# One activation instruction for a feed-forward's gate in 109 of its 256 units, tanh and a product in the other 147

## The chip, the cores and the metric

The kernel runs on one core of a Trainium2 chip. The metric is the device time of one execution in microseconds; the time before is the median of three runs. Five engines work side by side, each with its own queue of instructions and each waiting on the others through semaphores: PE (TensorE, the matmuls; PEld is its weight load), DVE (VectorE), ACT (ScalarE), POOL (GpSimd) and SP (SyncE, which here only issues DMAs).

## The reference

Three stages follow each other, all in float32:

```python
def _attn_ref(q, k, v, p):            # 8 batches, 8 heads, 576 tokens, head size 64
    p_packed = sm_attn(p, k, v)       # 32 packed queries
    return sm_attn(q, p_packed, p_packed)

def _moe_ref(x, w_in, w_out):         # 4608 tokens, 512 -> 2048 -> 512
    h = x @ w_in
    g = h * (1.0 / (1.0 + np.exp(-1.702 * h)))
    return (g @ w_out).astype(np.float32)

def _moe2_ref(x, w1, w2, w3, w_out):  # 512 -> 768 -> 512
    h = np.maximum(np.maximum(x @ w1, x @ w2), x @ w3)
    return (h @ w_out).astype(np.float32)
```

The change is in the gate of `_moe_ref`, the line `g = h * sigmoid(1.702 h)`.

## The kernel before

Every float32 product is made of three matmuls on a high and a low part of each operand (`mm3`, lines 100 to 102, the line numbers that most matmuls carry in the profile). So each left or right side has to be split: a copy into a rounded high part on ACT, then a subtraction for the low part, mostly on DVE.

The first feed-forward is cut into 256 **units**. A unit `n` is one batch, one half of its 576 tokens (288 columns) and one of 16 chunks of 128 of the 2048 hidden values. Three functions work on it:

- `h_unit(n)`: six matmuls of 288 columns into a PSUM tile `h` (two buffers, tag `ph`), then tanh(0.851 h) on ACT into `t` (line 460), then `t = (t + 1) * h` on DVE (line 461). This is twice the gated value, since sigmoid(1.702 h) is half of one plus that tanh. The product is the last reader of `h`.
- `g_unit(n)`: `t` is copied into the high part of `g` on ACT (line 466), and the low part is the difference (line 468), on DVE, for units 0 and 1 on POOL.
- `out_unit(n)`: twelve matmuls of 288 columns, which add `g` times a piece of `w_out` to four PSUM banks `acc`. After the last unit of a run of chunks the banks go to `x2` with a factor of one half (lines 488, 492 and 494), and a finished `x2` is written to DRAM.

In the plan, `out_unit(n - 2)` follows `h_unit(n)`, so a `g` has about two units' time to get ready. The attention of later batches and the conversion of weights run in between: softmax takes exponentials on ACT (lines 259 and 340), and `convert_low` and `conv_late` take the bit patterns of the weights apart with several DVE operations and a Relu with a bias on ACT (lines 154 and 520).

`main` lists all steps with due times and runs them in that order; each engine's queue is then put in order when the kernel is built, so a queue is not simply the program's text. Some instructions are tied behind the latest one of a kind: `sums` and `split_lo` behind `latest["dve"]`, `split_hi` behind `latest["act"]`.

From about 800 us on the second feed-forward runs, which the change does not touch.

Of the kernel before, what the change touches and what calls it, by code (L numbers as in the profile page):

```python
# [12 lines left out]
AF = mybir.ActivationFunctionType  # L13
ALU = mybir.AluOpType
# [29 lines left out]
def tile_packed_attention_moe(  # L44
# [13 lines left out]
    nc = tc.nc  # L58
# [19 lines left out]
    def f(t):  # L78
        return t.bitcast(F32)
# [11 lines left out]
    def x_tile(name, dt=F32):  # L91
        return up.tile([P, 4 * HALF], dt, tag="x", bufs=4, name=name)
# [5 lines left out]
    def mm3(o, a, b, start, stop, more=False):  # L98
        (ah, al), (bh, bl) = a, b
        nc.tensor.matmul(o, al, bh, start=start, stop=False, skip_group_check=more)  # L100
        nc.tensor.matmul(o, ah, bl, start=False, stop=False, skip_group_check=more)  # L101
        nc.tensor.matmul(o, ah, bh, start=False, stop=stop, skip_group_check=more)  # L102
# [313 lines left out]
    gt, acc = {}, {}  # L416
    latest = {}
# [30 lines left out]
        start.setdefault((b, fc // 4), n)  # L448
    part = {}

    def h_unit(n):
        b, hf, fc = units[n]
        o = ps_h.tile([P, TB], F32, tag="ph", name=f"h_{n}")[:, :HALF]
        hs = slice(hf * HALF, hf * HALF + HALF)
        fs = slice(fc % 4 * P, fc % 4 * P + P)
        for g in range(2):
            w = pw[b, fc // 4][:, g]
            mm3(o, (w[:, 0, fs], w[:, 1, fs]), [t[:, hs] for t in at[b, g]], g == 0, g == 1)
        t = gp.tile([P, HALF], F32, tag="t", name=f"t_{n}")
        nc.scalar.activation(t, o, AF.Tanh, scale=0.5 * 1.702)  # L460
        nc.vector.scalar_tensor_tensor(out=t, in0=t, scalar=1.0, in1=o, op0=ALU.add, op1=ALU.mult)  # L461
        gt[n] = t

    def g_unit(n):
        g = gp.tile([P, 2, HALF], F32R, tag="g", name=f"g_{n}")
        latest["act"] = nc.scalar.copy(g[:, 0], gt[n])  # L466
        eng = nc.gpsimd if n < 2 else nc.vector
        latest["dve"] = eng.tensor_tensor(out=g[:, 1], in0=gt[n], in1=f(g[:, 0]), op=ALU.subtract)  # L468
        gt[n] = g

    def out_unit(n):
        b, hf, fc = units[n]
        w = wo[fc]
        g = gt.pop(n)
        for dc in range(KD):
            if n in first:
                acc[dc] = ps_c.tile([P, TB], F32, tag=f"c{dc}", name=f"acc_{n}_{dc}")
            ds_ = slice(dc * P, dc * P + P)
            o = acc[dc][:, :HALF]
            mm3(o, (w[:, 0, ds_], w[:, 1, ds_]), (g[:, 0], g[:, 1]), n in first, n in last)  # L480
            if n not in last:
                continue
            if dc == 0:
                old = part.pop((b, hf), None)
                x2 = old or x_tile(f"x2_{n}")
                x2 = x2.rearrange("p (c t) -> p c t", c=KD)
            if old is not None:
                nc.vector.scalar_tensor_tensor(
                    out=x2[:, dc], in0=o, scalar=0.5, in1=x2[:, dc], op0=ALU.mult, op1=ALU.add
                )  # L490
            elif dc % 2 == 0:
                nc.scalar.mul(x2[:, dc], o, 0.5)
            else:
                nc.vector.tensor_scalar(out=x2[:, dc], in0=o, scalar1=0.5, scalar2=None, op0=ALU.mult)
        if n in last:
            if fc < NFC - 1:
                part[b, hf] = x2.rearrange("p c t -> p (c t)")
            else:
                c0 = b * S + hf * HALF
                nc.sync.dma_start(x2d[:, :, c0:c0 + HALF], x2)  # L500
# [303 lines left out]
    def main():  # L804
# [12 lines left out]
        for n in range(N1 + 2):  # L817
            tn[n] = t
            if n < N1:
                add(t, h_unit, n)  # L820
            if n >= 2:
                add(t + HU / 2, out_unit, n - 2)
            if n < N1:
                add(t + HU / 2 + .01, g_unit, n)
            t += (1.23 * HU) if n < 11 else HU * 1.16
# [181 lines left out]
```

## Time and profile before

| | us |
|---|---|
| median of three runs (1333.99 to 1334.6) | 1334.4 |
| the profiled execution's own time | 1333.64 |
| its span, first to last instruction | 1331.5 |
| PE busy in the span | 1308.8 |
| DVE busy in the span | 919.9 |
| ACT busy in the span | 533.3 |

The profile is one execution. Busy time is the union of an engine's instructions. A matmul of 288 columns is shown as some 0.3 us long, but they are pipelined, and one starts every 0.13 us; so PE can be shown busy while its queue loses a tenth of a microsecond, and losses are better read from the starts of its matmuls.

### The profile page before, as it was taken

The numbers are of one execution on the slowest core, as the hardware profiler recorded it, in microseconds if no ns is written. First come the engines' busy times: TensorE is split into PE (matmuls) and PEld (weight loads), VectorE is DVE, ScalarE is ACT, GpSimd is POOL, SyncE is SP. The second block draws the span as 40 slices with busy tenths as digits, with TensorE's granted clock in tenths as the row PEclk, the third lists the DMA queues.
The fourth block names the chain that finished last, engine by engine and source line by source line (L and its number), as shares of the span: only waits on it lengthen the run. The fifth ranks groups of instructions, "written<-read, shape, count | busy, mean of one in ns | idle before, by whom it ended". The sixth has DMA issues, their size and how long they took to land.

```text
span 1331.5 us, 22347 instructions
## 1 busy us (share of the span) xinstructions
PE 1308.8 (98%) x8614; PEld 1229.7 (92%) x8614; DVE 919.9 (69%) x1896; ACT 533.3 (40%) x1140; POOL 107.4 (8%) x218
## 2 busy tenths in 40 slices
PE   6899999999999999999999999999999999999998
PEld 5699898989999989999999999999899899999997
DVE  6899976874756565669999889736556467366461
ACT  3466544554445444446656442311311313123111
POOL 1200001100000000000000001001011011010000
PEclk9899999999999999999999999999999999999999
DMA  9697734643323331236655649847657476575451
GB/s 338 211 403 300 251 107 139 193 123 120 106 80 100 103 102 54 82 112 195 207 200 191 206 160 360 294 169 252 223 188 264 151 261 239 172 254 197 174 174 48
DMA packets 88875, 249.70 MB, mean 188 GB/s; under 512 B 10177, under 2 KB 39361, under 8 KB 81857
## 3 DMA queue, kind: packets, MB, share of 16 engines
q0 software_dynamic: 24640, 132.66, 29.2%
q1 hardware_dynamic: 64128, 115.62, 25.4%
q8 instruction: 68, 1.11, 0.3%
q14 instruction: 39, 0.31, 0.1%
HBM read 204.47 MB, written 43.78 MB: 186 GB/s over the span
## 4 chain that ended last, share of the span: by engine, by line
PE 92%; DVE 4%; DMA 2%; issue 1%; ACT 1%; SPq 0%; POOL 0%; ACTq 0%; DVEq 0%; POOLq 0%
PE acc L100 10%; PE p L101 10%; PE p L100 10%; PE p L102 10%; PE acc L102 10%; PE acc L101 9%; PE h L100 5%; PE h L102 5%; PE h L101 5%; PE accb L101 4%; PE accb L102 4%; PE accb L100 4%; PE pw L100 1%; PE pw L101 1%; PE pw L102 1%; PE pv L287 1%
## 5 line engine op out<-in xcount | busy, mean ns | idle before, releaser
L100 PE MATMUL acc<-g,wo 128*128 128x288 f32 x1024 | 303.6, 299 | 0.0
L102 PE MATMUL acc<-g,wo 128*128 128x288 f32 x1024 | 300.6, 294 | 0.0
L101 PE MATMUL acc<-g,wo 128*128 128x288 f32 x1024 | 299.6, 293 | 0.4 <-POOL g L468 0.3
L100 PEld LDWEIGHTS acc<-g,wo 128*128 128x128 f32 x1024 | 191.4, 188 | 10.5 <-issue 5.3
L101 PEld LDWEIGHTS acc<-g,wo 128*128 128x128 f32 x1024 | 192.2, 188 | 4.3 <-issue 1.0
L102 PEld LDWEIGHTS acc<-g,wo 128*128 128x128 f32 x1024 | 192.0, 188 | 1.6 <-issue 1.5
L460 ACT ACTIVATE t<-h 128x288 f32<-128x288 f32 x256 | 104.8, 410 | 181.7 <-PE h L102 179.8
L461 DVE SCALAR_TENSOR_TENSOR t<-t,h 128x288 f32<-128x288 f32 x256 | 114.7, 450 | 84.7 <-ACT t L460 83.3
L100 PE MATMUL h<-at,pw 128*128 128x288 f32 x512 | 155.2, 304 | 1.3 <-DVE t L461 1.1
L101 PE MATMUL h<-at,pw 128*128 128x288 f32 x512 | 151.7, 296 | 0.3 <-POOL at L125 0.3
L102 PE MATMUL h<-at,pw 128*128 128x288 f32 x512 | 151.3, 296 | 0.0
L466 ACT CAST g<-t 128x288 fp32r<-128x288 f32 x256 | 110.6, 433 | 93.6 <-DVE t L461 92.4
L468 DVE TENSOR_TENSOR g<-t,g 128x288 fp32r<-128x288 f32 x254 | 114.9, 453 | 34.7 <-ACT g L466 33.8
L681 DVE TENSOR_TENSOR u<-s,p 128x384 f32<-128x384 f32 x54 | 29.9, 553 | 119.1 <-PE p L102 119.1
L101 PE MATMUL p<-x_T,ws 128*128 128x384 f32 x324 | 108.2, 334 | 0.0
L100 PE MATMUL p<-x_T,ws 128*128 128x384 f32 x324 | 108.2, 334 | 0.0
L102 PE MATMUL p<-x_T,ws 128*128 128x384 f32 x324 | 108.1, 334 | 0.0
L100 PEld LDWEIGHTS h<-at,pw 128*128 128x128 f32 x512 | 96.3, 188 | 9.7 <-issue 5.6
L101 PEld LDWEIGHTS h<-at,pw 128*128 128x128 f32 x512 | 96.4, 188 | 1.7 <-POOL at L125 1.3
L102 PEld LDWEIGHTS h<-at,pw 128*128 128x128 f32 x512 | 96.4, 188 | 0.1
L711 ACT COPY s<-p 128x384 f32<-128x384 f32 x54 | 25.9, 479 | 161.8 <-PE p L102 161.7
L129 DVE TENSOR_TENSOR pw<-pw,pw 64x512 fp32r<-64x512 f32 (+1 forms) x110 | 74.9, 686 | 18.2 <-ACT pw L128 17.2
(175 smaller groups left out, 2637.1 us busy)
## 6 DMA issues: line engine op xcount, KB each, us to landing
ws<-wss POOLq DMA_DIRECT2D x54, 1024.0 KB, 7.6
wa<-wsa POOLq DMA_DIRECT2D x54, 768.0 KB, 4.6
wi<-wsc POOLq DMA_DIRECT2D x48, 512.0 KB, 3.9
k<-in_k SPq DMA_DIRECT2D x16, 576.0 KB, 4.2
q<-in_q SPq DMA_DIRECT2D x16, 576.0 KB, 3.9
x2d<-x SPq DMA_DIRECT2D x16, 576.0 KB, 4.0
wss<-ws SPq DMA_DIRECT2D x36, 256.0 KB, 4.0
xr<-x2d SPq DMA_DIRECT2D x24, 384.0 KB, 4.1
```

The costliest lines, as they stand in the source:

```text
L100: nc.tensor.matmul(o, al, bh, start=start, stop=False, skip_group_check=more)
L101: nc.tensor.matmul(o, ah, bl, start=False, stop=False, skip_group_check=more)
L102: nc.tensor.matmul(o, ah, bh, start=False, stop=stop, skip_group_check=more)
L129: nc.vector.tensor_tensor(out=lo, in0=o, in1=f(hi), op=ALU.subtract)
L287: self.mm = nc.tensor.matmul(o[x * D:x * D + D, :P], self.et[:, c * P + x * D:c * P + x * D + D], self.v[:, c, y * P:y * P + P], start=c = ...
L460: nc.scalar.activation(t, o, AF.Tanh, scale=0.5 * 1.702)
L461: nc.vector.scalar_tensor_tensor(out=t, in0=t, scalar=1.0, in1=o, op0=ALU.add, op1=ALU.mult)
L466: latest["act"] = nc.scalar.copy(g[:, 0], gt[n])
L468: latest["dve"] = eng.tensor_tensor(out=g[:, 1], in0=gt[n], in1=f(g[:, 0]), op=ALU.subtract)
L681: latest["dve"] = nc.vector.tensor_tensor(out=o, in0=a, in1=b, op=op)
L711: latest["act"] = nc.scalar.copy(self.s1, self.b1)
```

## The change

A unit is called direct when `10 <= n < 29`, `115 <= n < 129` or `n >= 180`: 19, 14 and 76 units, 109 of 256.

- In a direct unit, line 460 becomes one activation instruction whose function is h times sigmoid(1.702 h), and the DVE product of line 461 is not issued. `g_unit` copies and subtracts as before.
- In the other units `t` is still twice the gated value; the half is now applied in `g_unit`: the copy is a multiplication by 0.5 on ACT, and the subtraction a scalar-tensor-tensor operation on DVE.
- The factor of one half at `x2` goes: a scalar-tensor-tensor becomes a tensor-tensor addition, a multiplication by a constant becomes a copy.
- The low parts of units 0 and 1 move from POOL to DVE.
- `latest["act"]` is also set by the activation of a direct unit.

```diff
+    def direct(n):
+        return 10 <= n < 29 or 115 <= n < 129 or n >= 180
...
         t = gp.tile([P, HALF], F32, tag="t", name=f"t_{n}")
-        nc.scalar.activation(t, o, AF.Tanh, scale=0.5 * 1.702)
-        nc.vector.scalar_tensor_tensor(out=t, in0=t, scalar=1.0, in1=o, op0=ALU.add, op1=ALU.mult)
+        if direct(n):
+            latest["act"] = nc.scalar.activation(t, o, AF.Gelu_apprx_sigmoid)
+        else:
+            nc.scalar.activation(t, o, AF.Tanh, scale=0.5 * 1.702)
+            nc.vector.scalar_tensor_tensor(out=t, in0=t, scalar=1.0, in1=o, op0=ALU.add, op1=ALU.mult)
...
-        latest["act"] = nc.scalar.copy(g[:, 0], gt[n])
-        eng = nc.gpsimd if n < 2 else nc.vector
-        latest["dve"] = eng.tensor_tensor(out=g[:, 1], in0=gt[n], in1=f(g[:, 0]), op=ALU.subtract)
+        if direct(n):
+            latest["act"] = nc.scalar.copy(g[:, 0], gt[n])
+            latest["dve"] = nc.vector.tensor_tensor(out=g[:, 1], in0=gt[n], in1=f(g[:, 0]), op=ALU.subtract)
+        else:
+            latest["act"] = nc.scalar.mul(g[:, 0], gt[n], 0.5)
+            latest["dve"] = nc.vector.scalar_tensor_tensor(
+                out=g[:, 1], in0=gt[n], scalar=0.5, in1=f(g[:, 0]), op0=ALU.mult, op1=ALU.subtract
+            )
...
-                nc.vector.scalar_tensor_tensor(
-                    out=x2[:, dc], in0=o, scalar=0.5, in1=x2[:, dc], op0=ALU.mult, op1=ALU.add
-                )
+                nc.vector.tensor_tensor(out=x2[:, dc], in0=o, in1=x2[:, dc], op=ALU.add)
             elif dc % 2 == 0:
-                nc.scalar.mul(x2[:, dc], o, 0.5)
+                nc.scalar.copy(x2[:, dc], o)
             else:
-                nc.vector.tensor_scalar(out=x2[:, dc], in0=o, scalar1=0.5, scalar2=None, op0=ALU.mult)
+                nc.vector.tensor_copy(x2[:, dc], o)
```

## Rows read from the trace of the kernel before

**Rows 1.** The page's table of engines: busy us, share of the span, instructions.

```profile
PE 1308.8 (98%) x8614; PEld 1229.7 (92%) x8614; DVE 919.9 (69%) x1896; ACT 533.3 (40%) x1140; POOL 107.4 (8%) x218
...
PE 92%; DVE 4%; DMA 2%; issue 1%; ACT 1%; SPq 0%; POOL 0%; ACTq 0%; DVEq 0%; POOLq 0%
```

**Rows 2.** Busy time of each engine by stretch, with clock and DMA.

```profile
core 0: us, PE busy (x) PEld busy (x) DVE busy (x) ACT busy (x) POOL busy (x), PEclk, DMA share, GB/s
52.00:84.00 32.00, 30.63 (x211) 25.57 (x207) 30.26 (x57) 19.80 (x42) 8.35 (x9) 1.00 0.80 291
84.00:140.00 56.00, 55.98 (x393) 53.72 (x394) 52.38 (x95) 34.65 (x65) 3.63 (x5) 1.00 0.87 339
...
405.00:446.00 41.00, 41.00 (x299) 40.19 (x298) 24.52 (x50) 20.11 (x46) 3.18 (x6) 1.00 0.28 87
592.00:783.00 191.00, 189.82 (x1404) 187.05 (x1403) 181.18 (x428) 112.70 (x247) 4.78 (x9) 1.00 0.57 187
```

**Rows 3.** Timeline of 622 to 628 us, all engines.

```profile
624.27 0.41 ACT L460 ACTIVATE t<-h 128x288 f32<-128x288 f32 x1 [0.95 <-PE h L102]
...
625.46 0.29 PE L102 MATMUL acc<-g,wo 128*128 128x288 f32 x1
...
626.12 0.82 DVE L461 SCALAR_TENSOR_TENSOR t<-t,h 128x288 f32<-128x288 f32 x2
...
626.63 0.40 PE L100 MATMUL h<-at,pw 128*128 128x288 f32 x1 [0.88 <-DVE t L461]
...
626.87 0.29 PE L101 MATMUL h<-at,pw 128*128 128x288 f32 x1
...
627.00 0.29 PE L102 MATMUL h<-at,pw 128*128 128x288 f32 x1
```

**Rows 4.** PE's timeline, 617 to 618.5 us.

```profile
617.15 0.29 PE L102 MATMUL acc<-g,wo 128*128 128x288 f32 x1
617.66 0.40 PE L100 MATMUL h<-at,pw 128*128 128x288 f32 x1 [0.21 <-DVE t L461]
617.90 0.29 PE L101 MATMUL h<-at,pw 128*128 128x288 f32 x1
```

**Rows 5.** Groups of PE, matmuls of 512 columns, in 592:783, then in 405:446.

```profile
L101 PE MATMUL pw<-wi,sp 128*128 128x512 f32 x10 | 4.0, 396 | 0.0
...
L101 PE MATMUL pw<-wi,sp 128*128 128x512 f32 x6 | 2.4, 396 | 0.0
```

**Rows 6.** Groups by line and shape, whole span: busy us, mean ns, idle before.

```profile
L466 ACT CAST g<-t 128x288 fp32r<-128x288 f32 x256 | 110.6, 433 | 93.6 <-DVE t L461 92.4 <-PE acc L102 0.5
L460 ACT ACTIVATE t<-h 128x288 f32<-128x288 f32 x256 | 104.8, 410 | 181.7 <-PE h L102 179.8 <-ACT e L259 0.3
...
L468 DVE TENSOR_TENSOR g<-t,g 128x288 fp32r<-128x288 f32 x254 | 114.9, 453 | 34.7 <-ACT g L466 33.8
L461 DVE SCALAR_TENSOR_TENSOR t<-t,h 128x288 f32<-128x288 f32 x256 | 114.7, 450 | 84.7 <-ACT t L460 83.3
...
L488 DVE SCALAR_TENSOR_TENSOR x<-acc,x 128x288 f32<-128x288 f32 x56 | 22.5, 447 | 0.2
```

**Rows 7.** ACT's timeline at the start.

```profile
0.73 1.28 ACT L112 ACT_TABLE_LOAD   x1 [0.73 <-PEq L996]
2.11 0.31 ACT L112 ACTIVATE nident<-ident 128x128 fp32r<-128x128 f32 x1
```

**Rows 8.** ACT's timeline around 143 us, then 452 us, then 594 us.

```profile
143.52 0.41 ACT L460 ACTIVATE t<-h 128x288 f32<-128x288 f32 x1 [0.38 <-PE h L102]
143.82 0.50 ACT L259 ACTIVATE e<-s,st 128x288 f32<-128x288 f32 x1
...
452.61 0.51 ACT L259 ACTIVATE e<-s,st 128x288 f32<-128x288 f32 x1 [0.85 <-DVE st L254]
...
594.86 0.41 ACT L460 ACTIVATE t<-h 128x288 f32<-128x288 f32 x1
```

**Rows 9.** PE's timeline, 140 to 147 us.

```profile
144.06 0.29 PE L102 MATMUL acc<-g,wo 128*128 128x288 f32 x1
144.47 0.33 PE L273 MATMUL t<-ident,e 128*128 128x128 f32 x1
144.55 0.38 PE L100 MATMUL acc<-g,wo 128*128 128x288 f32 x1
```

**Rows 10.** Timelines of the start: POOL and PE at 57 us, PE at 84 us.

```profile
56.68 0.80 POOL L468 TENSOR_TENSOR g<-t,g 128x288 fp32r<-128x288 f32 x1 [0.60 <-ACT g L466]
...
57.53 0.40 PE L101 MATMUL acc<-g,wo 128*128 128x288 f32 x1 [0.33 <-POOL g L468]
...
84.02 0.50 PE L101 MATMUL pw<-wi,pt 128*128 128x512 f32 x1 [0.28 <-DVE wi L163]
```

**Rows 11.** A group of ACT in 592:783, the Relu of the weights' conversion.

```profile
L520 ACT ACTIVATE c<-c,rebias 128x512 int32<-128x512 int32 x16 | 11.6, 723 | 1.8 <-DVE c L519 1.4
```

## The prediction

> **What bounds the kernel now.** I read the page first, then busy time by stretch, then the waits of PE, then the timelines where PE lost time. The page says PE: busy 98% of the span, and 92% of the chain that ended last, with DVE at 4% [rows 1]. So an instruction taken from DVE or ACT is worth only what PE waits for it. The table by stretch tells how that differs over the three stretches of direct units: units 10 to 28 run at about 84 to 140 us, 115 to 128 at 405 to 446, and 180 to 255 at 592 to 783. DVE is busy 52.4 of 56 us in the first, 24.5 of 41 in the second and 181.2 of 191 in the third, the granted clock 1.00 (2.4 GHz) in all [rows 2]. The second has a slack DVE and a PE that never stands; there the change can only give what nobody waits for. In the third, DVE is late often enough for PE to notice.
>
> Because a matmul is shown longer than the 0.13 us at which they start (626.87 and 627.00 [rows 3]), PE's losses have to be estimated from counts. In 405:446, 299 matmuls, 18 of them 512 columns wide (three lines of 6 [rows 5]), took 41.00 us. With 0.130 to 0.132 us for a narrow one, a wide one comes to 0.25 to 0.22. At these paces the 1404 matmuls of 592:783 (29 wide, lines of 10, 10 and 9 [rows 5]) need 186.0 to 187.8 of 191 us, and the 393 of 84:140 (33 wide by the same view) 55.0 to 54.7 of 56 [rows 2]. So PE loses some 3.2 to 5.0 us in the third stretch and 1.0 to 1.3 in the first, from all causes together. That is an estimate, and the ceiling of what this change can give inside its stretches: about 6.
>
> **The change part by part.** *Removed: 109 products of line 461 at 450 ns [rows 6]*, 49 us of DVE, 34 of them in the third stretch. The visible loss they cause: an `acc` matmul starts at 625.46 and the next matmul of `h` at 626.63, 1.17 us instead of 0.13, with DVE's line 461 named; the activation of that unit had started at 624.27, and its product ran only at 626.12, behind weight conversion [rows 3]. The matmul after it starts 0.24 us later instead of 0.13, so a stop costs a further 0.11. That place costs 1.04 + 0.11 = 1.15; the one at 617, by the same reading, 0.38 + 0.11 = 0.49 [rows 4]. Sum 1.64. A direct unit frees its `h` when ACT is done, so both waits go. For the rest of that stretch I take 0.3 (between nothing and the 1.6 to 3.4 that the counts leave, nearer nothing, because no view names line 461 for it): **-1.9**. What is late next is ACT, 112.7 of 191 us busy [rows 2], with some 180 us of idle time ahead of its 256 activations of line 460 [rows 6], or the low part of `g`, still on DVE.
>
> In the first stretch DVE is as full, but the loss is 1.0 to 1.3 in all; I take **-0.3**, between 0 and -1.3. In the second, nothing.
>
> *Unchanged in price:* the gate activation in place of tanh (410 ns), the multiplying copy (433), the scalar-tensor-tensor in place of a subtraction (450 against 453), the addition at `x2` in place of the 447 of line 488 [rows 6]. If each of the 147 kept units' two edited operations took 10 ns more, it would be 3 us spread over engines that stand idle 5 to 41% of the third stretch [rows 2]; I take 0, ends 0 and 0.3 either way. The stricter `latest["act"]` can hold the ACT copy of `split_hi` behind one more activation of 0.41 us; its product is for weights of the second feed-forward, far ahead of need: 0.
>
> *Moved: the low parts of units 0 and 1 from POOL to DVE.* POOL's takes 0.80 us, and PE stands 0.33 for the first [rows 10]. On DVE it takes 0.45 once DVE is free, but DVE is busy 30.3 of 32 us from 52 to 84, and at 84.02 PE waits 0.28 for DVE's weight conversion of line 163 [rows 2, 10]. Two more operations ahead of that push it back by up to 0.9 us, less DVE's idle time before it. Bounds: -0.4 (the POOL waits gone, with a restart of PE) to +0.9. DVE being full, I take **+0.4**.
>
> *Added: table loads.* The kernel before has one, at the start, 1.28 us, and no second in spite of tanh, exp, Relu and copies [rows 7]; so those share a table. The new activation has not been seen in it. If it needs another, there are five more loads: into the gate's table for units 10, 115 and 180, and back before the exponentials at 143.82 and 452.61 [rows 8] (or before the tanh of units 29 and 129, if that is not in the new one). ACT has no product to wait for ahead of the load, so it can run in the idle time before an instruction. At 452.61 that is 0.85 us, and no transposition follows at once; at 594.86 ACT had none, but `h` has a second buffer [rows 8]. The exposed place is 143.82: ACT comes straight from a tanh, and PE's first transposition at 144.47 starts 0.41 us after an `acc` matmul instead of 0.13, 0.28 of standing behind that exponential [rows 8, 9]. A load there puts 1.28 on a chain that PE already waits for. But the same rows show one transposition inside a group of `acc` matmuls, as no line of the program orders it: the queues are filled by what is expected to be ready, and with a load expected, other matmuls can go first. Bounds: 0 to 5 x 1.28 = 6.4; I take **+0.4**, a third of one load.
>
> The next activation begins 0.10 us after the load's end [rows 7]. The Trainium skill (ScalarE: Activation LUTs, What ACT_TABLE_LOAD costs) gives 1283 ns for the load, which the row confirms, plus about 1380 ns of drain for every switch, 2.66 us in all; this trace, whose only load has no activation before it, cannot show the drain. By that page five switches are 13.3 us of ACT, and my term would be 0.9.
>
> *Sum:* -1.9 - 0.3 + 0.4 + 0.4 = -1.4 on the profiled execution's 1333.64 us (span 1331.5 and 2.1 around it): 1332.2. The median of the runs lies 0.76 above that execution, so in terms of runs **1333.0**.
>
> **The rivals.** A difference of 0.2%, 2.7 us, is about the least that can be told from none: below 1331.7 or above 1337.1.
>
> *The relief reaches further (faster).* If every wait on a full DVE vanishes, and the queues, refilled with 49 us less on DVE, also lose restarts of 0.11 us, most of the 3.2 to 5.0 and 1.0 to 1.3 goes: -4.2 to -6.3, with the additions of 0.8 -3.4 to -5.5, say -4: **1330.4**. For it: DVE at 95% of the third stretch. Against: PE's view names only two waits there. Chance 0.2.
>
> *The start eats it (same).* DVE carries the two products on its full stretch and PE pays 0.9, the load at 143.82 is paid whole, 1.28, and only the two visible waits go: +0.9 + 1.28 - 1.64 = +0.5, **1334.9**. For it: rows 8 to 10. Against: the queues can go round. Chance 0.2.
>
> *The loads land on PE's path (slower).* Place: the five switches, each with PE's matmuls waiting 1.28 us. All five: 6.4 - 1.64 = +4.8, **1339.2**. It decides from the fourth exposed load on (4 x 1.28 - 1.64 = 3.5, over 2.7). Against: at 86, 408 and 595 us `h` has a second buffer and `out_unit` runs two units behind. Chance 0.07.
>
> The page's 2.66 for a switch would make it decide at the second: 2 x 2.66 - 1.64 = 3.7, an estimate from the Trainium skill.
>
> *The Relu needs another table (slower, and not what the change says).* In the third stretch 16 Relus of line 520 run between direct units [rows 11], 22 with those of `w_out2`. If the gate's table lacked Relu, each would cost a load in and a load back, 2.56 us; with a unit every 2.4 us PE would pay perhaps 1 us of it each time: 22 less the gain of 1.4, **1355**. Against: one load has served tanh, exp, Relu and copies so far [rows 7]. Chance 0.03. The Trainium skill (same page, Table sets: the hidden batching unit) says that cheap functions such as relu and copy are in every set, which speaks the same way; nothing here shows it for this function.
>
> **How the numbers follow.** The forecast, small gain, has 0.5, with its own range 1331.8 to 1334.3. Of it and the start rival none leaves the band of no change; so faster 0.2, same 0.7, slower 0.1. The range from 1330.0 to 1336.8 leaves out the two slow rivals (0.1) and the far end of the fast one.
>
> **What would show it.** Right: 147 products on line 461's successor; no wait of PE's `h` matmuls on DVE in 592:783; DVE there down by 34 to about 147 us; five more loads of 1.28 us on ACT; PE busy the same. The start term is right if the matmul of `pw` at 84 us starts up to 0.9 later, the load term if the transposition at 144 us waits longer than before relative to its neighbours. Wrong: loads beyond five; PE waits for ACT's `t` or `g` in the third stretch; or an order of the queues so different that new waits for `wi` or attention appear elsewhere.

## The result: 18 us slower, and the profile after

The changed kernel takes 1352.4 us (median of 4 runs, 1349.2 to 1355.1) against 1334.5 of the kernel before on the same chip: a ratio of 1.0133 [1.0110, 1.0157], 18 us more. The profiled execution took 1355.1, its span is 1352.9. In the changed kernel lines from 451 on have moved down by 3 to 11: 460 and 461 are now 464 (direct) or 466 and 467, line 468 is 474 (direct) or 477, and the first operation of `conv_late`, line 519, is line 528.

The changed kernel's page, engines and then the shares of the chain that ended last:

```profile
PE 1311.9 (97%) x8614; PEld 1232.9 (91%) x8614; DVE 886.2 (66%) x1789; ACT 542.6 (40%) x1145; POOL 105.6 (8%) x216
...
PE 80%; DVE 8%; DMA 8%; issue 2%; SPq 1%; ACT 1%; POOL 0%; DVEq 0%; ACTq 0%; POOLq 0%
```

DVE has lost 107 instructions and 34 us, and 3 us more of PE's work are shown. Yet PE's share of the chain fell from 92% to 80%, DMA's rose from 2% to 8% and DVE's from 4% to 8% [rows 1]. Waits that hardly mattered before are now on the path to the end. Busy time by stretch says where:

```profile
core 0: us, PE busy (x) PEld busy (x) DVE busy (x) ACT busy (x) POOL busy (x), PEclk, DMA share, GB/s
52.00:84.00 32.00, 30.31 (x222) 25.59 (x223) 31.04 (x60) 18.45 (x41) 5.83 (x7) 1.00 0.79 291
84.00:143.00 59.00, 59.00 (x418) 56.33 (x418) 50.12 (x83) 40.80 (x71) 4.16 (x6) 1.00 0.88 341
409.00:450.00 41.00, 41.00 (x299) 40.19 (x299) 18.54 (x36) 21.51 (x46) 3.19 (x6) 1.00 0.31 91
597.00:805.00 208.00, 193.60 (x1396) 188.84 (x1395) 158.31 (x353) 113.65 (x247) 4.26 (x8) 0.98 0.53 171
```

The second stretch is the same to the digit for PE, 299 matmuls in 41.00 us [rows 2]. The third needs 208 us where it needed 191, PE stands 14.4 of them, and its mean granted clock is no longer 1.00. DVE, which was to be relieved, is now idle a quarter of the stretch. What it, ACT and PE wait for in 590:810 (engine and line, what it waited for, us in total, times, longest):

```profile
DVE c L528 <- DMA wraw<-in_w: 21.7, 13, 3.0
ACT c L529 <- DVE c L528: 20.6, 13, 5.4
DVE g L474 <- ACT g L473: 15.5, 12, 1.9
DVE c_o L528 <- DMA wraw_o<-in_w_out: 5.0, 5, 2.0
...
PE acc L100 <- ACT x L501: 4.9, 3, 2.6
PE acc L101 <- DVE g L474: 2.3, 2, 1.5
PE h L100 <- ACT t L464: 2.2, 3, 1.1
PE pw L100 <- issue: 2.2, 1, 2.2
PE acc L100 <- DVE x L503: 2.0, 2, 1.7
```

The same view of the kernel before:

```profile
DVE c L519 <- DMA wraw<-in_w: 1.3, 1, 1.3
...
PE h L100 <- DVE t L461: 1.1, 2, 0.9
```

PE's wait for the gate's product is gone, as forecast. But DVE stands 26.7 us at line 528 for raw weights that are still on their way, eighteen times, where it stood 1.3 us once. The low parts of `g` and the emptying of `acc` (line 503) stand behind it in DVE's queue, and PE waits for them: together the four waits of PE that name DVE come to 4.3 us, and seven that name ACT to 8.0 (0.9 of it for `g`, not shown). ACT in its turn stood 20.6 us for line 528. One such place, DVE's, PE's and SP's rows of the timeline (start, length, instruction, idle time before it and what ended it):

```profile
636.00 0.55 SPq L553 DMA_DIRECT2D wraw<-in_w  x1
636.60 1.50 SPq L555 DMA_DIRECT2D wraw<-in_w  x2
...
638.46 0.29 PE L102 MATMUL h<-at,pw 128*128 128x288 f32 x1
...
641.31 0.40 PE L100 MATMUL acc<-g,wo 128*128 128x288 f32 x1 [2.57 <-ACT x L501]
...
642.72 0.43 DVE L528 TENSOR_SCALAR c<-wraw 128x512 int32<-128x512 int32 x1 [1.98 <-DMA wraw<-in_w]
643.18 0.46 DVE L503 COPY x<-acc 128x288 f32<-128x288 f32 x1
...
643.69 0.52 PE L100 MATMUL acc<-g,wo 128*128 128x288 f32 x1 [1.72 <-DVE x L503]
644.01 0.44 PE L101 MATMUL acc<-g,wo 128*128 128x288 f32 x1
644.25 0.44 PE L102 MATMUL acc<-g,wo 128*128 128x288 f32 x1
```

DVE reaches line 528 some 2 us before the weights, whose load was issued at 636.0 to 638.1. The copy that empties a bank of `acc` is next in its queue, and PE's matmul at 643.69 waits for that copy. The stop before it, 2.57 us, names ACT's copy of another bank: ACT's queue had stood 3.05 us for DVE's line 129, the low part of `pw`. DVE was busy without a stop from 632.66 to the end of that operation at 639.40, mostly with conversion, so this first stop is not DVE's standing for weights. After the two stops the matmuls start 0.24 us apart instead of 0.13: the granted clock has fallen to its lower level (1.2 GHz), as the windows after it show.

```profile
643.60:647.20 3.60, 3.51 (x15) 3.51 (x16) 3.60 (x9) 1.04 (x3) 0.00 (x0) 0.53 0.43 153
647.20:665.00 17.80, 17.80 (x133) 17.61 (x133) 14.83 (x35) 10.24 (x23) 0.53 (x1) 1.00 0.63 202
```

In the kernel before, two loads were issued at 623.26 and 630.18, and their conversions came at 634.45 and 637.39, without a wait:

```profile
630.18 0.55 SPq L544 DMA_DIRECT2D wraw<-in_w  x1
630.78 1.14 SPq L546 DMA_DIRECT2D wraw<-in_w  x2
...
634.45 0.42 DVE L519 TENSOR_SCALAR c<-wraw 128x512 int32<-128x512 int32 x1
...
637.39 0.42 DVE L519 TENSOR_SCALAR c<-wraw 128x512 int32<-128x512 int32 x1
```

Over the first eight loads of the stretch the time from issue to conversion was 4.4 to 11.8 us, median 8.0, in the kernel before, with one wait for the landing; in the changed one 4.2 to 7.5, median 6.3, with six. The transfers were not slower: from issue to landing the eight took 4.1 to 7.2 us before (median 5.9) and 4.0 to 7.5 (median 6.1) in the changed kernel.

Why does DVE come too early? No line of the changed functions touches the conversions; what moved is their *place in DVE's queue*. The due times of the steps are the same, but each queue is put in order when the kernel is built, and with less work DVE can be expected to be free earlier there. That reason is an inference; the new places are counted. Counted in the traces, as the number of low parts of `g` that stand ahead of a late conversion's first operation (conversions 1 to 24, in order):

```
before  180 183 185 187 194 195 200 201 207 208 213 217 218 223 225 228 230 233 234 237 239 241 256 256
after   180 180 184 187 190 193 197 199 203 206 210 213 216 220 223 226 227 230 231 233 236 237 256 256
```

From the fifth to the 22nd they stand 2 to 4 places earlier, and a place is a unit, some 2.5 us (191 us for 76). That is the theory to be tested: **the queue's order, made for a DVE with less work, puts conversions ahead of the landing of their weights; DVE stands, and all that is behind it.** The rivals: the **loads** of the activation table cost the time; or the **instructions themselves** do (the direct activation, the new forms of the edited operations).

### The profile page after: what moved, and what is told of

It reads as the page before. It is cut to its first block, busy times and chain, and to the rows that moved or that the text cites. A ratio compares the mean times of both kernels' runs of the same rounds, so it can differ in the third digit from the quotient of the medians.

```text
span 1352.9 us, 22160 instructions
## 1 busy us (share of the span) xinstructions
PE 1311.9 (97%) x8614; PEld 1232.9 (91%) x8614; DVE 886.2 (66%) x1789; ACT 542.6 (40%) x1145; POOL 105.6 (8%) x216
## 4 chain that ended last, share of the span: by engine, by line
PE 80%; DVE 8%; DMA 8%; issue 2%; SPq 1%; ACT 1%; POOL 0%; DVEq 0%; ACTq 0%; POOLq 0%
PE p L100 10%; PE p L101 10%; PE p L102 10%; PE acc L100 8%; PE acc L102 7%; PE acc L101 7%; PE h L100 4%; PE h L101 4%; PE accb L101 4%; PE accb L102 4%; PE accb L100 4%; PE h L102 4%; DMA wraw<-in_w 3%; DMA wraw_o<-in_w_out 1%; PE pv L287 1%
## 5 line engine op out<-in xcount | busy, mean ns | idle before, releaser
L466 ACT ACTIVATE t<-h 128x288 f32<-128x288 f32 x147 | 60.4, 411 | 131.1 <-PE h L102 130.2
L467 DVE SCALAR_TENSOR_TENSOR t<-t,h 128x288 f32<-128x288 f32 x147 | 66.3, 452 | 68.1 <-ACT t L466 67.1
L129 DVE TENSOR_TENSOR pw<-pw,pw 64x512 fp32r<-64x512 f32 (+1 forms) x110 | 75.1, 687 | 19.6 <-ACT pw L128 18.3
L477 DVE SCALAR_TENSOR_TENSOR g<-t,g 128x288 fp32r<-128x288 f32 x147 | 66.1, 450 | 29.2 <-ACT g L476 28.5
L102 PE MATMUL accb<-wo,g 128*128 128x512 f32 x216 | 84.1, 390 | 0.0
```

The lines of the kernel that those rows point to most:

```text
L129: nc.vector.tensor_tensor(out=lo, in0=o, in1=f(hi), op=ALU.subtract)
L477: latest["dve"] = nc.vector.scalar_tensor_tensor(out=g[:, 1], in0=gt[n], scalar=0.5, in1=f(g[:, 0]), op0=ALU.mult, op1=ALU.subtract)
```

## The experiments

Each kernel was compared with the kernel before on the same chip (median 1333.7 to 1334.4). The *lag* of a unit below is the start of its first `h` matmul less the start of the same matmul in the kernel before, each from its span's start, in the profiled executions; the last column is that of the end of the second feed-forward (its last matmul of `accb`).

```
lag in us of unit     0     29     32    180    255    end of second feed-forward
after               1.8    1.2    4.6    3.6   22.2   21.8
third_only         -0.1   -1.0   -1.0   -1.5   17.5   17.1
first_two          -0.5   -0.9    2.6    1.6    1.9    1.9
no_direct          -0.5   -0.2   -0.2   -0.7    0.7    0.8
same_dve           -0.1   -0.5   -0.5   -0.3    6.7    6.3
held               -0.4   -1.0    2.5    2.1    7.4   16.9
held_all            1.6   -1.5    4.8    5.5    6.0   15.1
load_early         -0.4   -0.7    3.0    2.2   16.5   16.1
loads_only          1.6    1.5    1.5    1.4    1.2    1.2
loads_five          0.0   -0.1   -0.2    1.0    4.9    4.9
held_body           0.0    0.3    0.3    0.0    0.6    0.2
held_body_all       0.4    0.6    4.0    3.2    4.3    3.9
```

Except in loads_only, unit 0 comes before any edited instruction can act, and the kernels agree on DVE's order until about 57 us; its lag of -0.5 to 1.8 is what one execution differs from another. Each row is one execution: that of held is the slowest of its runs, 6 us above their median, that of same_dve the fastest, 2 below. The changed kernel loses 3.4 us between units 29 and 32 and 18.6 between 180 and 255, and nothing elsewhere.

### Which stretch: third_only, first_two, no_direct

```diff
-        return 10 <= n < 29 or 115 <= n < 129 or n >= 180
+        return n >= 180                               # third_only
+        return 10 <= n < 29 or 115 <= n < 129         # first_two
+        return False                                  # no_direct
```

> Only units 180 to 255 are direct; two loads fewer on each side of the first two stretches, so one load is added instead of five. Queue theory (DVE's freed time lets weight conversion be queued ahead of its raw weights' landing, and DVE stands): most of the loss stays, +12 to +18 us over the kernel before, DVE waiting over 20 us for wraw between 590 and 810. Load theory (the five table loads and what stands behind them): four fifths of the loss goes, under +5 us. Start theory (two low parts moved to DVE): +2 to +4 only at the start, the rest gone.

Measured: 1348.2, ratio 1.0100 [1.0079, 1.0122].

> Units 10 to 28 and 115 to 128 are direct, 180 to 255 take tanh and the product. Queue theory: the third stretch is as before, DVE's wait for wraw falls from 22 to under 3 us; left are the places at the start and near 143 us, +2 to +5 us in all. Load theory: four of the five loads are still there, +12 us or more.

Measured: 1335.6, 1.0011 [1.0001, 1.0020].

> No unit is direct: left are the half moved into g, the copies at x2, and the low parts of units 0 and 1 on DVE; one table load. Queue theory and load theory: -1 to +2 us. Start theory: +2 to +4 us, PE later by that much already at unit 30.

Measured: 1332.8, 0.9990 [0.9981, 0.9999].

The third stretch carries most of the loss: 13.9 of 17.9 us by the medians, all of it by the lags. Its queue in third_only has the same places as in the changed kernel, and its DVE the same waits:

```profile
DVE c L528 <- DMA wraw<-in_w: 22.3, 14, 3.2
...
DVE c_o L528 <- DMA wraw_o<-in_w_out: 3.7, 4, 1.8
```

The rest of the change, with all 256 units on tanh, the new halving operations and the low parts of units 0 and 1 on DVE, costs nothing: no_direct. So the instructions of the kept units are cleared. What first_two pays is one place, and the rows there look like the same mechanism in `convert_low` (lines 153 and 156); held_all, below, does not bear that out. DVE's rows there:

```profile
137.46 0.69 DVE L153 TENSOR_SCALAR raw_wo<-raw_wo 128x1024 int32<-128x1024 int32 x1
...
140.02 0.70 DVE L156 TENSOR_SCALAR low_wo<-low_wo 128x1024 int32<-128x1024 int32 x1 [1.87 <-DMA low_wo<-in_w_out]
...
143.23 0.20 DVE L254 TENSOR_SCALAR st<-st 128x1 f32<-128x1 f32 x1
```

In the kernel before these two operations ran at 145.06 and 145.73, behind the softmax's line 254. Here they stand ahead of it, the second waits 1.87 us for its weights, and PE waits 2.1 us for line 254. The clock granted over 140:146 is 0.86 on average.

### Is it the free time on DVE: same_dve

DVE gets the product's time back in the direct units, with an operation that leaves `t` as it is:

```diff
             latest["act"] = nc.scalar.activation(t, o, AF.Gelu_apprx_sigmoid)
+            nc.vector.scalar_tensor_tensor(out=t, in0=t, scalar=1.0, in1=t, op0=ALU.mult, op1=ALU.max)
```

> The changed kernel with a DVE operation of the same kind and size, t = max(1.0 * t, t), behind each direct activation, which leaves the values as they are: the gate, the five loads and the earlier release of h stay, DVE's time is not freed. Queue theory: the third stretch stands as before, DVE's wait for wraw under 5 us, in all -1 to +5 us over the kernel before. Load theory: +12 us or more as with the changed kernel.

Measured: 1342.2, 1.0060 [1.0039, 1.0081], between what the two theories expected. DVE's wait for raw weights falls from 26.7 to 3.6 us, and the loss of the third stretch from 18.6 to 7.0:

```profile
DVE c L529 <- DMA wraw<-in_w: 3.6, 4, 1.5
...
PE acc L101 <- DVE g L475: 1.8, 3, 0.8
PE acc L100 <- DVE x L504: 1.1, 2, 0.9
```

The direct activation is in all its units here, and more than half of the loss is gone: 109 *added* operations of 0.45 us on DVE make the kernel faster than the changed one. The places lie between those of before and after (190, 195, 198, 201, 204, ... from the fifth conversion on), so the order is not wholly back, and 7 us stay.

### Is it the load's time: load_early

```diff
-                (-8 if idx > 1 else -TP_[0] + .2, pc.load), (0, pc.conv), ...
+                (-11 if idx > 1 else -TP_[0] + .2, pc.load), (0, pc.conv), ...
```

> The changed kernel with the late raw weights due 11 us instead of 8 ahead of their conversion, still two buffers. If the wait for wraw is only a matter of when the load is asked for, DVE's wait falls by half and the time by 5 us or more; if the load cannot start before the buffer of two pieces earlier is free and SP's queue reaches it, or conversion is queued that much earlier too, it stays at +12 to +18 us.

Measured: 1349.0, 1.0120 [1.0102, 1.0137]. No help: DVE's wait at line 528 for `wraw` is still 19.6 us in 13 places, against 21.7, and the conversions have the places of the changed kernel. The earlier due time does not give the weights more time: over the first eight loads the median from issue to conversion is 5.7 us, against 6.3. There are two raw buffers, so a load also needs one to be free; a third was not tried.

### The table loads: loads_only, loads_five

The kernel before, with a small activation of the new kind and no other edit. In loads_only it reads a constant, in loads_five a column of the unit's `h`:

```diff
+        if n in (10, 115, 180):
+            nc.scalar.activation(tiny, rebias, AF.Gelu_apprx_sigmoid)      # loads_only
+            nc.scalar.activation(tiny, o[:, :1], AF.Gelu_apprx_sigmoid)    # loads_five
         nc.scalar.activation(t, o, AF.Tanh, scale=0.5 * 1.702)
```

> The kernel before, with tanh and the product everywhere, and an activation of one column with the new function ahead of the tanh of units 10, 115 and 180, so that the same five table loads happen on ACT with DVE as full as before. Load theory: +10 us or more. Queue theory: -1 to +3 us.

Measured: 1334.3, 1.0000 [0.9990, 1.0009]. A miss as a test: the small activations depend on nothing, so all three ran at the start, and there are two extra loads, at 2.44 and 11.97 us, which leave the time as it was.

> The kernel before with tanh and the product everywhere; ahead of the tanh of units 10, 115 and 180 one column of h goes through the new function, so that the three loads for it come there and the two back before the exponentials of 144 and 453 us (in loads_only these activations waited for nothing and ran at the start). Load theory: +10 us or more. Queue theory: -0.5 to +3 us, the most at 144 us.

Measured: 1337.6, 1.0024 [1.0015, 1.0033], +3.3 us. Here the five loads stand in the places of the changed kernel:

```profile
L462 ACT ACT_TABLE_LOAD x3 | 3.8, 1283 | 0.1
L260 ACT ACT_TABLE_LOAD x2 | 2.6, 1283 | 0.8 <-DVE st L255 0.8
```

The one at 143 us costs nothing by unit 32 (lag -0.2). Of the 4.9 us, 3.9 come between units 180 and 255, 3.8 of them by unit 190, right behind the third load. But they are not simply that load's time. In this kernel too the build has moved the first late conversions (places 180, 180, 184, 188, 190, then as before), and the second one meets its weights still on their way. The product behind it is late for PE, and the lag goes from 1.0 at unit 181 to 3.2 at unit 182:

```profile
600.74 0.43 DVE L522 TENSOR_SCALAR c<-wraw 128x512 int32<-128x512 int32 x1 [1.49 <-DMA wraw<-in_w]
601.20 0.46 DVE L464 SCALAR_TENSOR_TENSOR t<-t,h 128x288 f32<-128x288 f32 x1
...
601.71 0.40 PE L100 MATMUL h<-at,pw 128*128 128x288 f32 x1 [1.97 <-DVE t L464]
```

So the run meant to price the loads shows the queue's order at work once more, moved here by an activation that gives DVE no less to do. It leaves the loads some 3 of the 18 us at most, their effect on the order included, and third_only, with one switch in place of five, loses as much in its stretch as the whole change.

### Holding the conversions back: held, held_all, held_body, held_body_all

The direct test: the change as it is, but each late conversion tied behind the low part of `g` that precedes it in the program, so that it cannot move up.

```diff
 # held
         def conv(self):
             self.hl = [c_tile(f"wa{y}_{self.n}") for y in range(2)]
-            self.v, self.s = conv_late(self.n, self.raw, *self.hl, TB)
+            with tc.issue_after(latest["dve"].ins):
+                self.v, self.s = conv_late(self.n, self.raw, *self.hl, TB)
 # conv_wo2 likewise; held_all: from unit 10 on also lines 153 and 156
```

> The changed kernel with the DVE operations of each late weight conversion (line 528 and those after it) queued behind the latest low part of g at the conversion's due time; nothing else. Queue theory: it is the place of line 528 in DVE's queue that costs the third stretch its time; DVE's wait for wraw falls from 22 under 5 us and the stretch comes within 3 us of the kernel before, in all +1 to +5 us (the first stretch keeps its loss). If raw weights are late for another reason (DMA time or SP's queue), the stretch keeps 10 us or more.

Measured: 1343.7 (five runs, 1337.9 to 1350.0), 1.0059 [1.0038, 1.0081].

> As held, and also the conversion of the first feed-forward's weights from unit 10 on (lines 153 and 156). Queue theory: the loss between units 29 and 32 goes too, which is PE behind DVE behind the landing of low_wo; -2 to +2 us against the kernel before. Load theory for that place (the table load before the exponentials of 145 us): the 2 us there stay.

Measured: 1347.6, 1.0103 [1.0088, 1.0118].

Both are slower than expected. In the third stretch the hold works: no late conversion waits for its raw weights, and the stretch loses 5.3 us in held and 0.5 in held_all where the change lost 18.6. In held a stop like the first of those above is left, with no wait for weights near it; its cause is open:

```profile
636.63 0.40 PE L100 MATMUL acc<-g,wo 128*128 128x288 f32 x1 [2.61 <-ACT x L501]
```

In the first stretch the hold of held_all fails. DVE waits for no weights of lines 153 and 156 between 84 and 165 us, yet the lag goes from -1.5 at unit 29 to 4.8 at unit 32 and is 5.5 at unit 180. PE waits there for another operation of DVE, the addition at `x2`:

```profile
PE acc L100 <- DVE x L500: 2.2, 3, 1.3
```

So the cause of the first stretch's loss is not shown; the table load ahead of the exponentials, which is in every kernel with that stretch direct, is not ruled out as a part of it, though in loads_five, where DVE's order is another, it cost nothing by unit 32.

Both kernels also lose 9 to 10 us right behind the third stretch, at the start of the second feed-forward. The last four pieces are tied to the last low parts of `g` there, and their conversions come too late; two of their first operations in held:

```profile
788.65 0.42 DVE L528 TENSOR_SCALAR c<-wraw 128x512 int32<-128x512 int32 x1
...
798.28 0.42 DVE L528 TENSOR_SCALAR c<-wraw 128x512 int32<-128x512 int32 x1
```

In the kernel before, the corresponding conversions ran at 745.31 and 748.80. So the hold has to leave these four free:

```diff
+            if 2 * self.k + self.kc >= 14:
+                self.v, self.s = conv_late(self.n, self.raw, *self.hl, TB)
+                return
             with tc.issue_after(latest["dve"].ins):
 # held_body: direct for n >= 180 only; held_body_all: direct in all three stretches
```

> Only units 180 to 255 are direct, and the conversions of the first 14 late pieces and of w_out2 are queued behind the latest low part of g; the last four pieces are free. To be set beside third_only. Queue theory: neither DVE's wait for wraw in the third stretch nor the loss that held showed at the start of the second feed-forward (its last pieces had been queued behind the last g); 1331 to 1338 us. If the last pieces are not the cause of that second loss, 8 to 10 us of it stay, 1342 or more.

Measured: 1333.4 (12 runs against 1334.4), 0.9996 [0.9987, 1.0005].

> The changed kernel, all three stretches direct, with the queue order of held_body (first 14 late pieces and w_out2 behind the latest low part of g). Queue theory: the third stretch stays within 2 us of the kernel before, and what is left is the first stretch with its loads, about what first_two showed, +1 to +3 us: 1335 to 1338. If the five loads cost more once they are all there, 1339 or more.

Measured: 1335.3 (11 runs against 1333.7), 1.0007 [0.9998, 1.0016].

The conversions now stand at 181, 184, 188, 191, 194, 198, ..., 239, 240, within four places of those before, and DVE waits for no raw weight at all. DVE's longest wait and the busy times over 590:810 in held_body, then the busy times of the kernel before:

```profile
DVE g L474 <- ACT g L473: 25.1, 22, 1.9
...
590.00:810.00 220.00, 218.03 (x1579) 215.51 (x1579) 183.83 (x409) 125.05 (x263) 10.18 (x19) 1.00 0.62 208
590.00:810.00 220.00, 218.82 (x1580) 215.96 (x1579) 207.01 (x486) 120.83 (x262) 10.07 (x19) 1.00 0.62 208
```

PE runs 1579 matmuls there at a full clock, 1580 in the kernel before and 1483 in the changed one. Set against third_only, which has the same direct units and only lacks the tie, 14.8 us are back. That settles that the place of the late conversions in DVE's queue carries the loss of the third stretch. In held_body_all, 3.4 us stay between units 29 and 32.

The order of the conversions and the wait in front of them, over all kernels with direct units in the third stretch, with loads_five and first_two beside them:

```
                 wait of late conversions for weights, us    lag gained in third stretch, us
before                        1.3                                  -
after                        26.7                                 18.6
third_only                   26.0                                 19.0
same_dve                      3.6                                  7.0
held                          0.0                                  5.3
held_all                      0.0                                  0.5
load_early                   22.4                                 14.3
loads_five                    2.9                                  3.9
first_two                     1.4                                  0.3
held_body                     0.0                                  0.6
held_body_all                 0.0                                  1.1
```

The two columns go together at the ends, not in the middle: same_dve and held lose 5 to 7 us with little or no such wait. How the 18.6 us divide between DVE's standing and operations queued behind conversion work is not shown.

## Why the prediction was wrong

**The step that failed** is the term of -1.9 for the third stretch. It let the two visible waits go, and then named what is late next as "ACT" or "the low part of `g`, still on DVE". It kept every other instruction in its old place. But the queue is put in order at build, and with 109 products gone from it conversions that need a DMA moved up; where one stood for its weights, everything behind it in DVE's queue stood too, as the copy of 643.18 did. The text had seen such reordering twice (the transposition inside a group of `acc` matmuls at 144 us, and "other matmuls can go first") and both times counted it as a help; its last sentence allowed for "an order of the queues so different that new waits ... appear elsewhere", without a rival or a price. Measured, the term is +18.6 instead of -1.9; with the conversions held, +0.6 in held_body and +1.1 in held_body_all. So even without the harm the gain of 1.9 did not show in the stretch, though PE's wait for line 461 is gone in both. These are single executions, and the ratio's interval for held_body, [0.9987, 1.0005], does not exclude the forecast sum of -1.4, a ratio of 0.9990.

**First stretch** (-0.3 predicted): +3.4 in the changed kernel, between units 29 and 32. A wait of DVE for weights stands there, but taking it away in held_all did not take the loss away, so the cause is open. **Second** (0): 299 matmuls in 41.00 us, as before.

**Edited operations of the kept units** (0) and **the start** (+0.4): no_direct holds both, and its ratio is 0.9990 [0.9981, 0.9999]; the lag at unit 29 is -0.2. Right for the first, and the second not seen.

**Table loads** (+0.4, bounds 0 to 6.4). Five there are, of 1.28 us each, at the units foretold and ahead of the exponentials; none at a tanh of a kept unit, none at a Relu. So the fourth rival, Relu in another table, is out. One reading in the term is wrong: the loads did not use the idle time ahead of the exponentials. At 456.28 ACT stood 0.82 us for line 254 first and then took the load, as at 145.49. What the loads cost by themselves is not isolated: the +3.3 of loads_five lies inside the bounds, but 2.2 us came in one place through a conversion that the build had moved up, and in held_body, with a load at 594.86, the stretch loses 0.6.

**What would show it.** Over the same work, 590:810 in the kernel before and in held_body, DVE's busy time fell by 23 us (207.0 to 183.8), not by the 34 foretold, and over the whole changed kernel by 34, not 49. The forecast multiplied a count by the length of one operation; but neighbouring operations on DVE overlap in the profile (643.18 and 643.55, the first 0.46 long), and busy time is a union. The 147 products are on line 467, five loads are there, and `h` waits for DVE are gone. Of the signs of being wrong two came: in 590:810 of the changed kernel PE waits 2.2 us for ACT's `t` and 0.9 for ACT's `g`, and the order of the queues brought new waits, for `wraw`.

What stays open: 7 us of same_dve's third stretch. Its conversions stand up to four places early, but DVE's wait for weights is only 3.6 us in it. Open too are the loss of the first stretch, the 5.3 us of held, and why held varied over 12 us from run to run.

## What to carry to other kernels

Where an engine's queue is ordered at build, relief on that engine can change the order, and so can an instruction added elsewhere: list what can move up into the freed time, and ask of each such instruction when its input lands, above all if it is a DMA's. Here a full engine was what kept a prefetch ahead of its reader; tie the reader to an event of the main loop before taking work off, and leave out of the tie what belongs behind the loop. A count of places in the queue, before against after, together with the new waits on DMAs, shows where to look.

## What the runs showed of the hardware

**A switch of the activation table took 1.28 us and no more.** Rows of the changed kernel, into the new table and back:

```profile
87.02 1.28 ACT L464 ACT_TABLE_LOAD   x1 [0.36 <-PE h L102]
88.31 0.41 ACT L464 ACTIVATE t<-h 128x288 f32<-128x288 f32 x1
...
145.21 0.20 DVE L254 TENSOR_SCALAR st<-st 128x1 f32<-128x1 f32 x1
145.49 1.28 ACT L259 ACT_TABLE_LOAD   x1 [0.17 <-DVE st L254]
146.78 0.50 ACT L259 ACTIVATE e<-s,st 128x288 f32<-128x288 f32 x1
...
456.28 1.28 ACT L259 ACT_TABLE_LOAD   x1 [0.82 <-DVE st L254]
```

The activation begins 0.01 us after the load has ended, and ACT stood 0.36 and 0.17 us ahead of the load. Both loads back began 0.08 us after line 254, whose result the exponential reads, had ended (145.41 and 456.20): the load stood behind that wait. The Trainium skill (ScalarE: Activation LUTs, What ACT_TABLE_LOAD costs) adds a drain of about 1380 ns to every switch; these rows have no room for one, and the measurement decides.

**Two stops of PE cost more than their length.** After stops of 2.57 and 1.72 us the granted clock was 0.53 over 3.6 us, the level of 1.2 GHz, in which 15 matmuls started, one each 0.24 us. At 0.13 us they would have taken 2.0, so that clock took another 1.6 us behind 4.3 us of standing.
